# A fifth head-sum term moved from TensorE to GpSimd, and the value head sums in five batches

## The chip, the cores and the metric

The kernel runs on one core of a Trainium2 chip. The core has five engines with a queue of their own each: TensorE (PE in the profile, with its weight loads as PEld), VectorE (DVE), ScalarE (ACT), GpSimd (POOL) and SyncE (SP, which only issues transfers). The metric is the device time in microseconds of one execution of the whole program; lower is better. Three executions of the kernel before took 267.02, 267.12 and 267.43 us, median 267.12 us. On this kernel about 0.2% (0.53 us) is what a measurement can tell from no change.

## The reference

Two layers share one input of 2048 rows of 640 numbers, and their results are added to it:

```python
xn = _layernorm(x, axis=-1)
qkv = (xn @ wqkv)                      # 32 heads of 20, for q, k and v
# each position looks at 8 positions: itself and 2, 4, ... 14 rows back
logits = einsum("bhsd,bhswd->bhsw", q, kg) * 20 ** -0.5   # rows before 0 masked
o = einsum("bhsw,bhswd->bhsd", softmax(logits), vg)
h = (xn @ w_gate) * (xn @ w_up)        # 640 -> 1536
return x + o @ wo + h @ w_down
```

The dense products fill TensorE. The local attention is elementwise work: for each of the 8 offsets, q is multiplied by the shifted k, and the 20 products of a head are summed.

## The kernel before, in words

The 2048 rows are cut into four blocks of 512 (`NJ = 4`, `JB = 512`), and the 640 columns into five chunks of 128 partitions (`NCH = 5`). Columns are permuted so that in every chunk four neighbouring partitions belong to one head; a head's 20 numbers are four partitions in each of five chunks.

**Logits.** The 8 offsets are two groups of four, `r = 1` and `r = 0`. For one block, one group and one chunk, VectorE writes a tile of products (`PRD`, 128 x 4 x 512 in bf16, line 879, in `narrow`). TensorE then sums over partitions with the 128 x 32 matrix `G`: each product tile costs four matmuls, one for each stretch of 128 rows, into four column strips of one PSUM bank (line 994, in `logits`). For blocks 0 and 1 all ten tiles of a block (five chunks, two groups) go this way, 40 matmuls a block. Blocks 2 and 3 (`QUAD`) are different: only chunk 4 is made by `narrow`; the chunks 0 to 3 are multiplied straight out of PSUM by VectorE into FP32 half tiles (`PRF`, 128 x 2 x 512, line 926, in `wide`; `q0` = 0 or 2 names the half), and these are added up before TensorE sees them. `sum32` adds one half to another, by a GpSimd instruction (line 952) or, for the pairs in `BY_DMA`, by a transfer that accumulates (line 948), and `close` adds the last two and writes a bf16 half (line 970). So one group of a block gives two tiles to TensorE, the sum of four chunks and chunk 4 alone: four tiles a block. Blocks 2 and 3 are summed in one go (`JOIN`), 32 matmuls.

**Softmax** runs over pairs of blocks, on VectorE with the exponential on ScalarE (`softmax`, lines 1027 to 1054).

**Values.** For each unit `u` (block j, chunk c; 20 units), VectorE multiplies the shifted values by the weights (line 1173), GpSimd adds pairs of offsets (line 1178, two instructions a unit, tile `SV`), and TensorE sums the four groups of 32 partitions with `SEL` (line 1231, four matmuls a unit, in `sums`). The head sums are made in batches of five units, after unit 4, 9, 14 and 19 (`BATCH`). ScalarE copies the result to `OT`.

**Dense layers.** `gu` multiplies by the gate and up weights, for each block twelve pairs of five matmuls (line 1287); the two halves are multiplied by VectorE (lines 1296 and 1334). `dn` multiplies by the down weights and adds the attention's output product, 12 and 5 matmuls for each piece of 320 columns (line 1389). Units of block j must be summed before the pieces of block j can end.

**What sets the order.** Nothing runs dynamically. A planner (`Sched`) runs when the program is built: each step is a `Task` with an engine, a priority, the PSUM banks that it needs and the banks that must stay free beside them (`keep`). The planner has an assumed duration for each step and places the step that can start first on its engine, by priority. What comes out is one fixed order for each engine, with semaphore waits between them. So a change to a priority, a `keep` or an assumed duration changes the order of instructions on several engines. `GU_KEEP = 3` banks are held back from the gate and up products and `DN_KEEP = 5` from the down products, for the head sums. VectorE instructions whose operands all lie in SBUF and GpSimd's additions are kept apart in time (`lock=True`).

Of the kernel before, what the change touches and what calls it, by code (L numbers as in the profile page):

```python
# [11 lines left out]
NCH = 5  # L12
# [37 lines left out]
class Sched:  # L50
# [184 lines left out]
    def run(self):  # L235
        while self.threads:
            alive = []
            i = 0
            while i < len(self.threads):
                th = self.threads[i]  # L240
                if th[1] is not None or self._advance(th):
                    alive.append(th)
                i += 1
            self.threads = alive
            best = {}
            free = sorted((t, b) for b, t in self.banks.items() if t is not None)
            for th in self.threads:
                k = th[1]
                if k is None:
                    continue  # L250
                if k.banks and k.banks + k.keep > len(free):
                    continue
                got = self.choose(k, free)
                if k.banks and not got:
                    continue
                s = max([self.t[k.eng], k.ready] + [self.banks[b] for b in got])
                if k.lock:
                    s = max(s, self.t_lock)
                best.setdefault(k.eng, []).append((s, k, th))
            if not best:  # L260
                if self.threads:
                    raise RuntimeError(f"stuck: {len(self.threads)} threads at {self.t} banks {self.banks}")
                break
            pick = None
            for eng, c in best.items():
                lim = max(self.t[eng], min(x[0] for x in c)) + self.PATIENCE[eng]
                x = min((x for x in c if x[0] <= lim), key=lambda x: (x[1].prio, x[1].seq))
                if pick is None or x[0] < pick[0]:
                    pick = x
            _, k, th = pick  # L270
            th[1] = None
            if k.banks:
                got = self.choose(k, free)
                for b in got:
                    self.banks[b] = None
                k.emit(*got)
            else:
                k.emit()
# [77 lines left out]
def build_kernel(nc, A_x, A_wqkv, A_wo, B_x, B_w_gate, B_w_up, B_w_down, out):  # L356
# [65 lines left out]
    PRD += [sb("PRD12", [128, 4, JB], at=a_sc), sb("PRD13", [128, 4, JB], at=a_sc + 4096)]  # L422
    PRD32 = [K.sbuf(f"PRF{i}", [128, 2, JB], FP32, K.base[p.name]) for i, p in enumerate(PRD)]
    QUAD = {2: (1, 0), 3: (1, 0)}
    BY_DMA = (((0, 0), (0, 2)), ((1, 0), (1, 2)))
    a_xr = place[0]
    FB0 = sb("FB0", [128, 5, D])
# [32 lines left out]
    def mark(*k):  # L460
        done.add(k)
# [4 lines left out]
    def have(*k):  # L466
        return lambda: k in done
# [367 lines left out]
    def tokens():  # L835
        return []
# [7 lines left out]
    def products():  # L844
        rows = {j: [] for j in range(NJ)}
        joined = []
        holds = {}
        for at, (j, kind) in enumerate(ORDER):
            if kind == "w":
                if j not in holds:  # L850
                    yield from fetch(j, 0, holds.setdefault(j, {c: [] for c in range(4)}))
                yield from wide(j, rows[j], holds[j])
            else:
                if len(QUAD.get(j, ())) == 2 and j not in holds and (j, "w") == ORDER[at + 1]:
                    yield from fetch(j, 0, holds.setdefault(j, {c: [] for c in range(4)}))
                for r in (1, 0):
                    for c in range(NCH - 1 if r in QUAD.get(j, ()) else 0, NCH):
                        yield from narrow(j, r, c, rows[j])
            if len(rows[j]) == 10 - 3 * len(QUAD.get(j, ())):
                if j in JOIN:  # L860
                    joined.append((j, rows[j]))
                    if len(joined) == len(JOIN):
                        K.spawn(logits(*joined))
                else:
                    K.spawn(logits((j, rows[j])))
        mark("products")
# [42 lines left out]
    def wide(j, slots, hold):  # L909
        halves = [(r, q0) for r in QUAD[j] for q0 in (0, 2)]  # L910
        acc, parts = {}, {1: [], 0: []}
        for c0 in (0, 2):
            for i, (r, q0) in enumerate(halves):
                f = []
                for c in (c0, c0 + 1):
                    yield lambda: len(hold[c]) > 0 and len(usable(j)) > 0
                    yield num(4, "qk", 0, j, c)
                    k = slot(j)
                    f.append(k)
                    o = PRD32[k]  # L920
                    kv, rk = k_view(j, r, c, q0, 2)
                    q = PS[:, hold[c][0], :]
                    qb = q.unsqueeze(1).to_broadcast([128, 2, JB])

                    def go(o=o, qb=qb, kv=kv, q=q, rk=rk):
                        X = op("dve", lambda e: e.tensor_tensor(o[:], qb, kv, ALU.mult), r=[q, rk, ("qev", j, c)], w=[o[:]],  # L926
                               name=f"prow{j}_{r}_{c}_{q0}", occ=1.17)
                        if c == 3:
                            mark("prow", j, r, q0)
                        if (r, q0) == halves[-1]:  # L930
                            K.free_bank(hold[c][0], X)

                    yield Task("dve", go, r=[q, rk], w=[o[:]], prio=20 + j)
                    if c == 2:
                        K.spawn(close(j, r, q0, acc, f, parts[r]))
                if c0 == 0:
                    acc[r, q0] = f[0]
                    K.spawn(sum32(j, r, q0, 0, *f))
                if i == len(halves) - 2 and c0 == 0:
                    yield from fetch(j, 2, hold)  # L940
        for r in QUAD[j]:
            slots.append((acc[r, 0], PRD[acc[r, 0]], r, parts[r]))

    def sum32(j, r, q0, p, a, b):
        x, y = PRD32[a][:], PRD32[b][:]
        name = f"qsum{j}_{r}_{q0}_{p}"
        if (r, q0) in BY_DMA[p]:
            yield Task("pool", lambda: op("pool", lambda e: e.dma_start(x, y, accum_op=ALU.add), r=[x, y], w=[x], dma=True,
                                          name=name, occ=0.88, acc=3.4), r=[x, y], w=[x], prio=4)
        else:  # L950
            yield calm
            yield Task("pool", lambda: op("pool", lambda e: e.tensor_tensor(x, x, y, ALU.add), r=[x, y] + tokens(), w=[x],  # L952
                                          name=name, occ=2.36, lock=True), r=[x, y], w=[x], prio=5, lock=True)
        free.append(b)

    def close(j, r, q0, acc, f, parts):
        A = acc[r, q0]
        a, x, o = PRD32[A][:], PRD32[f[0]][:], PRD[acc[r, 0]][:, q0:q0 + 2, :]
        if (r, q0) in BY_DMA[1]:
            yield have("prow", j, r, q0)  # L960
            yield from sum32(j, r, q0, 1, *f)
            y = x
        else:
            yield from sum32(j, r, q0, 1, A, f[0])
            yield have("prow", j, r, q0)
            y = PRD32[f[1]][:]
        if q0:
            yield lambda: len(parts) == 1
        yield calm
        yield Task("pool", lambda: op("pool", lambda e: e.tensor_tensor(o, a, y, ALU.add), r=[a, y] + tokens(), w=[o],  # L970
                                      name=f"qend{j}_{r}_{q0}", occ=2.36, lock=True), r=[a, y], w=[o], prio=5, lock=True)
        free.append(f[0] if (r, q0) in BY_DMA[1] else f[1])
        if q0:
            free.append(A)
        parts.append(q0)
# [108 lines left out]
        yield Task("sp", move, r=[L[:]], prio=4)  # L1084

    NU = NJ * NCH
    BATCH = (4, 9, 14, 19)

    def vx_loads():
        yield have("products")  # L1090
# [128 lines left out]
    def sums(us):  # L1219
# [5 lines left out]

        def go(*bs):
            hold.extend(bs)
            for u, b in zip(us, bs):
                for dq in range(4):
                    o, p = PS[32 * dq:32 * dq + 32, b, :], SV[sv_of[u]][:, dq, :]  # L1230
# [25 lines left out]
        return count.get(("lg",), 0) >= NJ and m < 11 and ucount[0] - count.get(("hp",), 0) < HP_MAX  # L1256

    SEQ = [(0, range(NF)), (1, range(6)), (2, (0, 1, 2, 3, 8, 9, 10, 11)), (1, range(6, NF)), (2, range(4, 8)), (3, range(NF))]

    def gu():  # L1260
        for m in range(NCH):
# [4 lines left out]
        for j, m in [(j, m) for j, ms in SEQ for m in ms]:  # L1266
# [73 lines left out]
                yield num(k0, "hf")  # L1340
                yield Task("dve", fmul, r=[h, us], prio=H_PRIO, lock=True)

            yield Task("pe", lambda b: go(0, b), prio=50, banks=1, keep=GU_KEEP, r=[WG[:]])
            K.spawn(after())
            yield Task("pe", lambda b: go(1, b), prio=49, banks=1, keep=GU_KEEP - 1, r=[WU[:]])
            bump("gus", j)
            if count["gus", j] == NF:
                mark("gu", j)
# [24 lines left out]
    def dn_piece(j, t, nb, rows, c0, c1):  # L1373
# [60 lines left out]
            if nb == 1:  # L1434
                mark("out", t)

        yield Task("pe", down, prio=41, banks=1, keep=0 if count.get(("ot", j), 0) >= NCH else DN_KEEP, r=[WD[:], WO[:]])
        K.spawn(tail())

    FAST = [(1, m) for m in range(6, NF)] + [(2, m) for m in range(4, 8)]  # L1440
# [11 lines left out]
    ORDER = ((0, "n"), (1, "n"), (2, "n"), (3, "n"), (2, "w"), (3, "w"))  # L1452
    LAST = ORDER[-1][0]
    HP_PRIO = 30
    DN_KEEP = 5
    H_PRIO = 9
    FIN_PRIO = 8

# [75 lines left out]
```

## Time and profile before

| | |
|---|---|
| median of three executions | 267.12 us (267.02 to 267.43) |
| profiled execution, first to last instruction (span) | 265.2 us, granted clock 1.000 |
| median less that span (start and end around it) | 1.9 us |
| VectorE busy | 220.0 us (83%) |
| GpSimd busy | 143.8 us (54%) |
| ScalarE busy | 111.8 us (42%) |

The profiled execution is an execution of its own; it is known by its span of 265.2 us, and its time is taken as that span and the 1.9 us around it. In the profile's timeline a row is a run of neighbouring instructions on one engine: the start, the length, the engine, the line, what is written and read, how many, and in brackets how long the engine had been idle and who ended that. In the table of groups, the columns behind the count are busy time, mean nanoseconds of one instruction, and idle time just before them. TensorE's matmuls overlap, so the length of a row is somewhat more than the distance to the next row's start; distances between starts are used below for what a row costs.

### The profile page before, as it was taken

The numbers are of one execution on the slowest core, as the hardware profiler recorded it, in microseconds if no ns is written. First come the engines' busy times: TensorE is split into PE (matmuls) and PEld (weight loads), VectorE is DVE, ScalarE is ACT, GpSimd is POOL, SyncE is SP. The second block draws the span as 40 slices with busy tenths as digits, with TensorE's granted clock in tenths as the row PEclk, the third lists the DMA queues.
The fourth block names the chain that finished last, engine by engine and source line by source line (L and its number), as shares of the span: only waits on it lengthen the run. The fifth ranks groups of instructions, "written<-read, shape, count | busy, mean of one in ns | idle before, by whom it ended". The sixth has DMA issues, their size and how long they took to land.

```text
span 265.2 us, 4403 instructions
## 1 busy us (share of the span) xinstructions
PE 259.5 (98%) x1748; PEld 152.5 (58%) x1764; DVE 220.0 (83%) x259; ACT 111.8 (42%) x203; POOL 143.8 (54%) x89
## 2 busy tenths in 40 slices
PE   7999999999999999999999999999999999999996
PEld 5996965444444444444444444477557755775675
DVE  4687899999998699667999999999999989992212
ACT  3559987556612211224267653511442144211300
POOL 3000000000644996169973476799999989997000
DMA  7974679960479994840069734453893657004211
GB/s 206 371 220 82 123 126 394 394 247 2 126 148 188 236 215 82 162 79 1 4 167 317 151 77 114 95 149 98 223 198 84 155 109 159 2 0 61 41 49 52
DMA packets 39685, 37.84 MB, mean 143 GB/s; under 512 B 15696, under 2 KB 37328, under 8 KB 39632
## 3 DMA queue, kind: packets, MB, share of 16 engines
q1 hardware_dynamic: 36688, 31.32, 44.0%
q0 software_dynamic: 2736, 6.16, 13.6%
q8 instruction: 14, 0.23, 0.4%
q10 hardware_dynamic: 240, 0.07, 0.1%
q14 instruction: 7, 0.06, 0.1%
HBM read 25.07 MB, written 7.23 MB: 122 GB/s over the span
## 4 chain that ended last, share of the span: by engine, by line
PE 89%; ACT 5%; DVE 3%; issue 2%; DMA 1%; DVEq 0%
PE PS L1287 37%; PE PS L1389 28%; PE PS L697 17%; ACT XNS L608 3%; PE PS L994 2%; PE PS L729 2%; PE PS L1231 1%; DVE PV L1173 1%; DMA XST<-in_A_x_dram 1%; DVE XNT L1296 1%; ACT QT L702 1%; ACT VST L702 1%; ACT KT L702 1%; PE PS L641 1%; ACT SD L583 0%
## 5 line engine op out<-in xcount | busy, mean ns | idle before, releaser
L1178 POOL TENSOR_TENSOR SV<-PV 128x1024 bf16<-128x1024 f32 x40 | 94.7, 2463 | 16.0 <-DVE HT L1334 7.8
L1173 DVE TENSOR_TENSOR PV<-VX,PS 128x1024 f32<-128x1024 bf16 (+1 forms) x54 | 90.6, 1725 | 0.6 <-POOL SV L1178 0.5
L697 PE MATMUL PS<-XNT,WQKV 128*128 128x512 bf16 (+2 forms) x384 | 60.0, 315 | 0.5 <-issue 0.3
L1287 PE MATMUL PS<-XNT,WU 128*128 128x512 bf16 x239 | 59.4, 379 | 0.1
L1287 PE MATMUL PS<-XNT,WG 128*128 128x512 bf16 x231 | 57.7, 379 | 0.6 <-issue 0.2
L697 PEld LDWEIGHTS PS<-XNT,WQKV 128*128 128x128 bf16 x390 | 37.8, 112 | 21.9 <-ACT LOG L1005 0.8
L1287 PEld LDWEIGHTS PS<-XNT,WU 128*128 128x128 bf16 x240 | 23.5, 98 | 28.1
L1287 PEld LDWEIGHTS PS<-XNT,WG 128*128 128x128 bf16 x240 | 23.4, 98 | 28.1 <-ACT LOG L1005 0.4
L926 DVE TENSOR_TENSOR PRF<-PS,KT 128x1024 f32<-128x1024 f32 x32 | 37.9, 1216 | 0.3 <-PE PS L697 0.3
L952 POOL TENSOR_TENSOR PRF<-PRF,PRF 128x1024 f32<-128x1024 f32 x8 | 18.8, 2358 | 21.6 <-DVE LOG L1054 20.6
L702 ACT ACTIVATE HT<-PS 128x512 bf16<-128x512 f32 x24 | 14.3, 596 | 35.3 <-PE PS L1287 35.3
L1389 PE MATMUL PS<-WD,HT 128*128 128x320 bf16 x192 | 28.4, 299 | 0.5 <-DVE XNT L1296 0.5
L702 ACT ACTIVATE FB<-PS 128x320 bf16<-128x320 f32 x24 | 10.5, 438 | 40.5 <-PE PS L1389 40.5
L879 DVE TENSOR_TENSOR PRD<-QT,KT 128x2048 bf16<-128x2048 bf16 x24 | 27.3, 1218 | 0.0
L1389 PE MATMUL PS<-WO,OT 128*128 128x320 bf16 (+2 forms) x165 | 26.3, 295 | 0.0
L1013 POOL MEMSET LOG<- 32x6 bf16 (+6 forms) x7 | 0.4, 95 | 43.8 <-ACT LOG L1005 43.8
L1389 PEld LDWEIGHTS PS<-WD,HT 128*128 128x128 bf16 x192 | 18.6, 98 | 8.5 <-DVE XNT L1296 1.0
L970 POOL TENSOR_TENSOR PRD<-PRF,PRF 128x1024 bf16<-128x1024 f32 x8 | 19.0, 2396 | 0.9 <-DVE PRF L926 0.8
L1389 PEld LDWEIGHTS PS<-WO,OT 128*128 128x128 bf16 x165 | 16.0, 98 | 5.8
L1296 DVE TENSOR_TENSOR HT<-HT,PS 128x512 bf16<-128x512 bf16 x18 | 12.3, 685 | 8.1 <-PE PS L1287 8.1
L1402 DVE TENSOR_TENSOR FB<-PS,XR 128x320 bf16<-128x320 f32 (+2 forms) x9 | 4.1, 455 | 14.9 <-PE PS L1389 14.9
L573 DVE BATCH_NORM_STATS2 STATS<-XST 128x6 f32<-128x320 bf16 x32 | 14.1, 470 | 2.2 <-DMA XST<-in_A_x_dram 2.2
(71 smaller groups left out, 233.4 us busy)
## 6 DMA issues: line engine op xcount, KB each, us to landing
VX<-v_scratch SPq DMA_DIRECT2D x80, 130.0 KB, 2.9
PRF<-PRF POOLq DMA_DIRECT2D x8, 512.0 KB, 4.9
XST<-in_A_x_dram SPq DMA_DIRECT2D x16, 160.0 KB, 5.6
v_scratch<-VST SPq DMA_DIRECT2D x4, 640.0 KB, 5.6
WG<-in_B_w_gate_dram SPq DMA_DIRECT2D x1, 1920.0 KB, 8.4
WU<-in_B_w_up_dram SPq DMA_DIRECT2D x1, 1920.0 KB, 12.0
out_dram<-in_A_x_dram SPq DMA_DIRECT2D x1, 1920.0 KB, 19.4
WD<-in_B_w_down_dram SPq DMA_DIRECT2D x1, 1920.0 KB, 8.7
```

The costliest lines, as they stand in the source:

```text
L573: op("dve", lambda e: e.bn_stats(o, a), r=[a], w=[("st", t, i)], name=f"bn{t}_{i}", occ=0.49)
L697: op("pe", (lambda o, l, x, c, first: lambda e: e.matmul(o, l, x, start=first, stop=(c == NCH - 1)))(o, l, x, c, first), r=[l, x], w=[o], ...
L702: X = op("act", (lambda o, i: lambda e: e.activation(o, i, ACT.Copy))(o, i), r=[i], w=[o], name=name, occ=0.12 + n * 0.9e-3)
L879: op("dve", lambda e: e.tensor_tensor(s[:], qb, kv, ALU.mult), r=[q, rk], w=[s[:]], name=f"prod{j}_{r}_{c}", occ=1.15, lock=True)
L926: X = op("dve", lambda e: e.tensor_tensor(o[:], qb, kv, ALU.mult), r=[q, rk, ("qev", j, c)], w=[o[:]], name=f"prow{j}_{r}_{c}_{q0}", occ=1.17)
L952: yield Task("pool", lambda: op("pool", lambda e: e.tensor_tensor(x, x, y, ALU.add), r=[x, y] + tokens(), w=[x], name=name, occ=2.36, lock ...
L970: yield Task("pool", lambda: op("pool", lambda e: e.tensor_tensor(o, a, y, ALU.add), r=[a, y] + tokens(), w=[o], name=f"qend{j}_{r}_{q0}", ...
L1173: last[0] = op("dve", lambda e: e.tensor_tensor(p, vw, a, ALU.mult), r=[vv] + rk, w=[p], name=f"pv{u}_{x}_{r0}", occ=0.09 + 1.1 * nr)
L1178: X = op("pool", lambda e: e.tensor_tensor(o, p[:, :, 0, :], p[:, :, 1, :], ALU.add), r=[p[:]] + tokens(), w=[o], name=f"pva{u}_{x}", occ= ...
L1287: op("pe", (lambda l, x, c: lambda e: e.matmul(PS[:, b, :], l, x, start=(c == 0), stop=(c == NCH - 1)))(l, x, c), r=[l, x], w=[PS[:, b, :] ...
L1296: X = op("dve", lambda e: e.tensor_tensor(h, h, PS[:, hold[1], :], ALU.mult), r=[h, PS[:, hold[1], :]], w=[h], name=f"h{m}_{j}", occ=0.65)
L1389: op("pe", (lambda l, x, i: lambda e: e.matmul(dst, l, x, start=(i == 0), stop=(i == n - 1)))(l, x, i), r=[l, x], w=[PS[:, b, :]], name=f" ...
```

## The change

Three things are changed.

1. In blocks 2 and 3 the product of chunk 4 no longer goes to TensorE as a tile of its own. `sum32` adds it, half by half, into the FP32 sum of chunks 0 and 1, by one more GpSimd addition (FP32 and bf16 in, FP32 out; `LAST_DMA` is empty, so none goes by transfer). `close` waits for it in the planner. There are eight such additions: two blocks, two groups, two halves. The head sums of blocks 2 and 3 then have one tile a group, 16 matmuls where there were 32.
2. `BATCH` has five entries: the last five units are summed as three (15, 16, 17) and two (18, 19).
3. The banks held back follow the head sums: `reserve` holds none back in some phases, and the down products keep as many banks free as the next batch has units (`next_sums`) in place of five.

In the built program GpSimd has eight instructions more, TensorE 16 matmuls fewer; VectorE, ScalarE and SyncE have the same instructions in another order. TensorE's order differs in four places: the order of one gate/up pair beside a group of line 697; the place of the 16 matmuls among the gate/up pairs of the second block, with as many pairs ahead of them as before; one gate group in the first two batches' wake ahead of the down products and its up group behind them; and at the end, where the three remaining gate/up groups come earlier, the batch of three stands before the down products of the last block, and the batch of two stands behind 36 of their matmuls (before: one batch of five behind 12).

```diff
@@ Sched.run
-                if k.banks and k.banks + k.keep > len(free):
+                if k.banks and k.banks + (k.keep() if callable(k.keep) else k.keep) > len(free):
@@ build_kernel
     QUAD = {2: (1, 0), 3: (1, 0)}
+    LAST_DMA = ()
     BY_DMA = (((0, 0), (0, 2)), ((1, 0), (1, 2)))
@@ products
-            if len(rows[j]) == 10 - 3 * len(QUAD.get(j, ())):
+            if len(rows[j]) == 10 - 4 * len(QUAD.get(j, ())) and kind == ("w" if j in QUAD else "n"):
@@ wide
         acc, parts = {}, {1: [], 0: []}
+        lastc = {r: [n, 0] for n, _, r in slots}
+        slots.clear()
...
-                    K.spawn(sum32(j, r, q0, 0, *f))
+                    K.spawn(sum32(j, r, q0, 0, *f, last=lastc[r]))
...
-    def sum32(j, r, q0, p, a, b):
+    def sum32(j, r, q0, p, a, b, last=None):
...
         free.append(b)
+        if last is None:
+            return
+        z = PRD[last[0]][:, q0:q0 + 2, :]
+        if (r, q0) in LAST_DMA:
+            yield Task("pool", lambda: op("pool", lambda e: e.dma_start(x, z, accum_op=ALU.add), r=[x, z], w=[x], dma=True,
+                                          name=name + "c", occ=0.88, acc=3.4), r=[x, z], w=[x], prio=4)
+        else:
+            yield calm
+            yield Task("pool", lambda: op("pool", lambda e: e.tensor_tensor(x, x, z, ALU.add), r=[x, z] + tokens(), w=[x],
+                                          name=name + "c", occ=2.36, lock=True), r=[x, z], w=[x], prio=5, lock=True)
+        last[1] += 1
+        mark("sum", j, r, q0)
+        if last[1] == 2:
+            free.append(last[0])
@@ close
         if q0:
             yield lambda: len(parts) == 1
+        yield have("sum", j, r, q0)
         yield calm
@@ build_kernel
-    BATCH = (4, 9, 14, 19)
+    BATCH = (4, 9, 14, 17, 19)
@@ sums, go
             hold.extend(bs)
+            bump("sums")
@@ build_kernel
+    def next_sums():
+        n = count.get(("sums",), 0)
+        return BATCH[n] - (BATCH[n - 1] if n else -1) if n < len(BATCH) else 0
+
+    def reserve(n):
+        k = sum(("add", u) in done for u in range(NU))
+        return 0 if k % 5 < 2 and k else n
@@ gu
-            yield Task("pe", lambda b: go(0, b), prio=50, banks=1, keep=GU_KEEP, r=[WG[:]])
+            yield Task("pe", lambda b: go(0, b), prio=50, banks=1, keep=lambda: reserve(GU_KEEP), r=[WG[:]])
             K.spawn(after())
-            yield Task("pe", lambda b: go(1, b), prio=49, banks=1, keep=GU_KEEP - 1, r=[WU[:]])
+            yield Task("pe", lambda b: go(1, b), prio=49, banks=1, keep=lambda: reserve(GU_KEEP) - 1 if reserve(GU_KEEP) else 0, r=[WU[:]])
@@ dn_piece
-        yield Task("pe", down, prio=41, banks=1, keep=0 if count.get(("ot", j), 0) >= NCH else DN_KEEP, r=[WD[:], WO[:]])
+        yield Task("pe", down, prio=41, banks=1, keep=0 if count.get(("ot", j), 0) >= NCH else next_sums, r=[WD[:], WO[:]])
@@ build_kernel
-    DN_KEEP = 5
```

## The prediction

> **What bounds the kernel now.** I read the page's busy shares first, then the chain that ended last, then the timelines of TensorE and GpSimd where the change lies. The busy shares and the clock:
>
> ```profile
> PE 259.5 (98%) x1748; PEld 152.5 (58%) x1764; DVE 220.0 (83%) x259; ACT 111.8 (42%) x203; POOL 143.8 (54%) x89
> core 0: 265.2 us, clock 1.000
> ```
>
> TensorE is the bound, at full clock: what is taken from its queue is gained, as long as nothing it waits for comes late. The chain, in order of time, shows the head sums of blocks 2 and 3 on it, and the one place behind them where TensorE isn't what ends last:
>
> ```profile
> 133.81 1.84 PE PS L994 x32
> ...
> 157.39 5.36 PE PS L1287 x24
> 162.75 0.66 DVE XNT L1296
> ...
> 169.05 0.69 DVE XNT L1296
> 169.74 0.05 issue
> 169.78 18.65 PE PS L1389 x136
> ```
>
> The reader is to see 32 matmuls in 1.84 us (0.0575 us each), and that from 162.75 to 169.74 VectorE sets the pace. TensorE's timeline shows what that is worth, and what a batch of value head sums costs:
>
> ```profile
> 168.06 1.26 PE L1231 MATMUL PS<-SV,SEL 128*32 128x512 bf16 x20
> 169.78 3.43 PE L1389 MATMUL PS<-WD,HT 128*128 128x320 bf16 x24 [0.46 <-DVE XNT L1296]
> ...
> 194.84 1.26 PE L1231 MATMUL PS<-SV,SEL 128*32 128x512 bf16 x20
> 196.03 3.43 PE L1389 MATMUL PS<-WD,HT 128*128 128x320 bf16 x24
> ...
> 244.65 1.26 PE L1231 MATMUL PS<-SV,SEL 128*32 128x512 bf16 x20
> 245.84 3.43 PE L1389 MATMUL PS<-WD,XNT 128*128 128x320 bf16 x24
> ```
>
> From start to start the batches at 194.84 and 244.65 take 1.19 us, that at 168.06 takes 1.72: 0.53 us is a wait. GpSimd's timeline shows what room the eight new additions find:
>
> ```profile
> 82.07 0.86 POOL L948 DMA_DIRECT2D PRF<-PRF  x1 [3.53 <-DVE PRF L926]
> ...
> 97.72 4.68 POOL L952 TENSOR_TENSOR PRF<-PRF,PRF 128x1024 f32<-128x1024 f32 x2
> 102.34 0.82 POOL L948 DMA_DIRECT2D PRF<-PRF  x1
> ...
> 114.45 0.86 POOL L948 DMA_DIRECT2D PRF<-PRF  x1 [5.62 <-DVE PRF L926]
> ...
> 127.92 2.35 POOL L970 TENSOR_TENSOR PRD<-PRF,PRF 128x1024 bf16<-128x1024 f32 x1
> 130.22 4.71 POOL L1178 TENSOR_TENSOR SV<-PV 128x1024 bf16<-128x1024 f32 x2
> ...
> 241.44 2.86 POOL L1178 TENSOR_TENSOR SV<-PV 128x1024 bf16<-128x1024 f32 x1
> ```
>
> **The change part by part.**
>
> *Matmuls removed.* 16 of line 994 at 0.0575 us, on TensorE, on the path: −0.92 us. Bounds: 0 if TensorE then waits for GpSimd there, 16 x 0.0575 otherwise. The stop and start around the group (0.09 us ahead of 133.74) stay.
>
> *Eight additions on GpSimd.* One distance is 2.31 us (97.72 to 102.34 is two): 18.5 us more work between 68.70 and 130.22. GpSimd's idle times in that stretch, all waits for VectorE's products, are 0.25, 2.25, 3.53, 0.83, 1.91, 2.05, 5.62 and 0.87: 17.3 us. If all of it is filled, GpSimd comes to the value additions 1.2 us later; if none, 18.5. The new additions stand in the order between the transfers and additions that did the waiting, so I am near the first: 1 us of waits stays for the first half tiles of block 3, which VectorE still makes when it did, and the shift is 2.2 us. Its cover, place by place:
> - The logits. The last `close` ended at 130.27 and ends at 132.5; TensorE reaches line 994 after as many matmuls as before, at 133.74. 1.2 us are left. If that cover goes, TensorE waits with all gate and up pairs queued behind it.
> - The softmax of the second pair follows the same evacuation on ScalarE, which doesn't move. VectorE's value products wait for `PV` buffers that GpSimd frees, 2.2 us later at first. From 130.22 to 169.21 GpSimd is idle 15.5 us (0.42, 4.35, 3.47, 1.74, 0.87, 0.61, 2.34, 1.65), mostly for VectorE multiplications kept apart from it, so the shift can be caught up there. TensorE reaches the first batch of value sums later itself: one more gate/up pair ahead of it, twice the 1.08 us from the group at 165.81 to that at 166.89, less 0.92: 169.3 instead of 168.06. GpSimd's additions for that batch ended at 167.56. If the shift is caught up, 1.7 us are left; if all of it were carried, TensorE would wait 0.5.
> - The last batch. From 169.21 on GpSimd has little idle time, so the shift may carry to its last addition, 244.30 + 2.2 = 246.5. TensorE came to that batch at 244.65, 18.3 us before its last matmuls began (262.9). Now 24 matmuls that stood behind it stand ahead (245.84 to 249.11, 3.27 us), and 12 value sums with them (0.69): 14.3 us before an end at 261.8, so 247.5. 1.0 us is left, against 0.35 before.
>
> So the additions cost nothing by this sum. Their duration is the unknown: an addition of FP32 and bf16 into FP32 is not in the trace. The rows around it:
>
> ```profile
> L970 POOL TENSOR_TENSOR PRD<-PRF,PRF 128x1024 bf16<-128x1024 f32 x8 | 19.0, 2396 | 0.9 <-DVE PRF L926 0.8
> L952 POOL TENSOR_TENSOR PRF<-PRF,PRF 128x1024 f32<-128x1024 f32 x8 | 18.8, 2358 | 21.6 <-DVE LOG L1054 20.6
> L926 DVE TENSOR_TENSOR PRF<-PS,KT 128x1024 f32<-128x1024 f32 x32 | 37.9, 1216 | 0.3 <-PE PS L697 0.3
> ```
>
> Between 2.35 (the shortest two-operand addition of the trace on GpSimd) and 2.87 (the longest, one with a transfer's issue beside it). I take 2358 ns, the row with the same output and first operand; the type of the output moves it by 38 ns. The lower end gains nothing, since GpSimd isn't the bound; the upper end is the rival that ends slower.
>
> The Trainium skill speaks against this part: GPSIMD Engine Reference, section "Engine selection", says to keep elementwise work on a tile off GpSimd, which is about twice as slow with two inputs. The rows agree on the ratio (2358 against 1216 ns for as many numbers on VectorE). By the page's 4497 ns for 2048 numbers, the eight would be an estimated 18.0 us and not 18.5, and the sum the same. The rule would make of the change a loss only where GpSimd's time is the path's; the 17.3 us idle say it isn't.
>
> *The wait at 169.78.* VectorE's last gate multiplication freed a bank 0.53 us late. Now a gate group stands ahead of the down products there, and TensorE arrives 1.24 us later, while VectorE has one more multiplication to do by then (0.6 us): 0.64 us of lateness taken off. That would clear all of 0.53, but VectorE's value products are themselves held by the later GpSimd. Ends: 0 and −0.53; I take −0.35.
>
> *The fifth batch.* A batch of 20 takes 1.19 us and its matmuls 1.15; with the 0.10 ahead of it (the up group at 193.66 would end its 1.08 at 194.74) a batch more costs 0.15 us. Ends: 0.05 and 0.25.
>
> *Banks held back and order.* The gate and up groups moved are the same matmuls, and a bank held longer by a lone gate group is one of eight. SyncE's order differs only in four value loads, of unit 6, that now stand behind the sixteen transfers of the second pair's attention weights and not ahead; VectorE needs unit 6 at 170.78, and those transfers were issued from 151.95 to 162.2; four loads and 2.9 us to landing end by 167, 3.8 us ahead of need. I cost this at nothing; its ends are the 0.53 that one late bank cost in this trace, either way.
>
> **Sum**: −0.92 − 0.35 + 0.15 = −1.12 us. The profiled execution's span goes from 265.2 to 264.1; with the same 1.9 us around it, the median from 267.12 to 266.0.
>
> **The rivals.**
> 1. *The new additions are longer than the FP32 ones and the logits wait (slower).* Cover at line 994 is 1.2 us, 0.15 for each of eight. From 2.51 us each TensorE waits; each further 0.1 costs 0.8 us; the 1.12 is gone at 2.65, and from 2.72 on the kernel is measurably slower. At 2.87 each: 8 x 0.51 − 1.2 = 2.9, so 268.9 us. For it: the form isn't in the trace. Against it: all three forms that are lie within 2.36 to 2.46 in the mean.
> 2. *GpSimd's shift is larger than 2.2 and shows at the first or last batch.* At 3.2 to 3.7 us of shift it costs 0.5 to 1 us: 266.5 to 267.0. For it: from 169 us on nothing is idle on GpSimd. Against it: 15.5 us idle ahead of that.
> 3. *New waits for banks or for VectorE.* Another order, with fewer banks held back, gives one or two waits of 0.53, and the old one stays: 267.0 to 267.8. For it: VectorE is busy 33.78 of the 36 us from 134 to 170. Against it: the batches at 194.84 and 244.65 show no wait now.
>
> **How the numbers follow.** Forecast 0.64 (its own range 265.7 to 266.4: the wait from 0 to −0.53, the batch from 0.05 to 0.25); rival 1 0.10; rival 2 0.18; rival 3 0.08. 0.2% is 0.53 us, what a measurement of this kernel can tell from no change. Faster: the forecast and 0.08 of rival 2, 0.72. Same: the rest of rival 2 and half of rival 3, 0.14. Slower: rival 1 and half of rival 3, 0.14. The range is 265.4 to 267.6: below, both order terms at their good ends (−0.92 − 0.53 + 0.05 − 0.3); above, rivals 2 and 3, with rival 1 left out.
>
> **What would show it.** Right: 16 matmuls in some 0.92 us at line 994 at the same start, without idle time before it that GpSimd ended; the new additions at 2.36 us; the first value addition at 132.4; no wait, or under 0.2, behind the first batch; the last value addition done before TensorE's batch at 247.5. Wrong: additions over 2.5 us, idle time before line 994 or 1231 put down to GpSimd, or a row of line 1389 or 1287 waiting for VectorE by more than 0.5 us.

## The result and the profile after

The changed kernel takes 266.25 us (median of 22 runs, 265.75 to 267.75) where the kernel before takes 267.21 us beside it (22 runs, 266.9 to 267.5). The ratio is 0.9972, with a 95% interval of 0.9964 to 0.998: faster by about 1.0 us. The prediction was 266.0 us.

A run's time has two parts, the span from first to last instruction and a rest around it. Before, the span is 265.5 us in the median of the 59 runs beside the experiments below, with a rest of 1.67 to 1.89. The changed kernel's 22 runs have a median span of 264.35, 21 of them from 264.0 to 264.6 and one 266.0, with a rest of 1.70 to 2.93. So most of the spread of its times lies outside the span. In spans it is 1.15 us faster.

The busy shares of the changed kernel:

```profile
PE 259.8 (98%) x1748; PEld 151.8 (57%) x1748; DVE 220.1 (83%) x259; ACT 111.9 (42%) x203; POOL 160.8 (61%) x97
core 0: 264.4 us, clock 1.000
```

GpSimd has 17.0 us more, VectorE and ScalarE are as they were, and the span is 0.8 us shorter. TensorE's count of matmuls reads 1748 in both profiles although 16 were taken out, so matmul records are missing from the trace of before (its weight loads read 1764, now 1748), and the sums below go by starts, not by busy time. The chain that ended last, in order of time, at the places that the prediction spoke of:

```profile
8.74 2.99 PE PS L730 x50
...
134.22 0.98 PE PS L1012 x16
...
169.83 1.19 PE PS L1250 x20
171.03 1.19 PE PS L1314 x5
172.21 18.47 PE PS L1416 x136
...
242.10 0.76 PE PS L1250 x12
242.86 5.00 PE PS L1416 x36
247.86 0.55 PE PS L1250 x8
248.40 13.75 PE PS L1416 x117
...
262.17 0.29 DVE FB L1429
```

Line 994 is now 1012: 16 matmuls in 0.98 us where there were 32 in 1.84. From 162.75 to 169.74, where VectorE set the pace before, there is now TensorE alone, and its first batch of value sums (line 1231, now 1250) is followed by the next matmul without a gap.

The first row shows what the span hides. TensorE's 50 matmuls of line 730 (729 before) began at 8.74, against 8.33 in the profile of before, because the second load of `x` landed late; that 0.41 us has nothing to do with the change. I therefore compare a stretch that leaves the start out, from the start of these 50 matmuls to the start of the last result on VectorE: 262.94 − 8.33 = 254.61 us before, 262.17 − 8.74 = 253.43 after, **1.18 us less**. "The stretch" below is this measure.

GpSimd's timeline around the new additions (line 966), the value additions (line 1196) and the end:

```profile
78.10 0.86 POOL L951 DMA_DIRECT2D PRF<-PRF  x1 [0.34 <-DVE PRF L929]
78.66 4.54 POOL L966 TENSOR_TENSOR PRF<-PRF,PRD 128x1024 f32<-128x1024 f32 x2
82.83 1.20 POOL L951 DMA_DIRECT2D PRF<-PRF  x1
83.44 2.75 POOL L966 TENSOR_TENSOR PRF<-PRF,PRD 128x1024 f32<-128x1024 f32 x1
85.53 2.96 POOL L955 TENSOR_TENSOR PRF<-PRF,PRF 128x1024 f32<-128x1024 f32 x1
87.84 2.95 POOL L988 TENSOR_TENSOR PRD<-PRF,PRF 128x1024 bf16<-128x1024 f32 x1
...
100.89 0.87 POOL L951 DMA_DIRECT2D PRF<-PRF  x1 [0.86 <-DVE PRF L929]
...
110.55 0.87 POOL L951 DMA_DIRECT2D PRF<-PRF  x1 [1.12 <-DVE PRF L929]
...
132.57 4.68 POOL L1196 TENSOR_TENSOR SV<-PV 128x1024 bf16<-128x1024 f32 x2
...
243.96 2.86 POOL L1196 TENSOR_TENSOR SV<-PV 128x1024 bf16<-128x1024 f32 x1
```

Of the 17.3 us that GpSimd waited for VectorE's products, 0.34 + 0.86 + 1.12 = 2.3 us are left; the additions lie in the rest. Its first value addition comes at 132.57 (130.22 before), and its last ends at 246.82, just before TensorE's last batch:

```profile
242.03 0.83 PE L1250 MATMUL PS<-SV,SEL 128*32 128x512 bf16 x12
242.80 5.06 PE L1416 MATMUL PS<-WD,XNT 128*128 128x320 bf16 x36
247.79 0.61 PE L1250 MATMUL PS<-SV,SEL 128*32 128x512 bf16 x8
```

### The profile page after: what moved, and what is told of

Same layout as the page of the kernel before. It is cut to its first block, busy times and chain, and to the rows that moved or that the text cites. A ratio compares the mean times of both kernels' runs of the same rounds, so it can differ in the third digit from the quotient of the medians.

```text
span 264.4 us, 4405 instructions
## 1 busy us (share of the span) xinstructions
PE 259.8 (98%) x1748; PEld 151.8 (57%) x1748; DVE 220.1 (83%) x259; ACT 111.9 (42%) x203; POOL 160.8 (61%) x97
## 4 chain that ended last, share of the span: by engine, by line
PE 96%; DMA 2%; DVE 1%; SPq 0%; ACT 0%; issue 0%
PE PS L1314 39%; PE PS L1416 28%; PE PS L698 23%; PE PS L1012 2%; PE PS L1250 2%; PE PS L730 2%; DMA XST<-in_A_x_dram 2%; DVE STATS L574 0%; PE PS L642 0%; SPq L480 0%; ACT XNT L655 0%; DVE XNS L603 0%; ACT SD L584 0%; DVE FB L1429 0%; DVE MV L577 0%
## 5 line engine op out<-in xcount | busy, mean ns | idle before, releaser
L698 PE MATMUL PS<-XNT,WQKV 128*128 128x512 bf16 (+2 forms) x390 | 60.8, 316 | 0.0
L1314 PE MATMUL PS<-XNT,WG 128*128 128x512 bf16 x240 | 59.7, 379 | 0.0
L955 POOL TENSOR_TENSOR PRF<-PRF,PRF 128x1024 f32<-128x1024 f32 x8 | 22.0, 2755 | 20.6 <-DVE LOG L1072 20.6
L988 POOL TENSOR_TENSOR PRD<-PRF,PRF 128x1024 bf16<-128x1024 f32 x8 | 21.5, 2768 | 0.1
L966 POOL TENSOR_TENSOR PRF<-PRF,PRD 128x1024 f32<-128x1024 f32 x8 | 19.5, 2543 | 0.0
```

The source lines that it names most:

```text
L698: op("pe", (lambda o, l, x, c, first: lambda e: e.matmul(o, l, x, start=first, stop=(c == NCH - 1)))(o, l, x, c, first), r=[l, x], w=[o], ...
L1314: op("pe", (lambda l, x, c: lambda e: e.matmul(PS[:, b, :], l, x, start=(c == 0), stop=(c == NCH - 1)))(l, x, c), r=[l, x], w=[PS[:, b, :] ...
```

## The experiments

My theory: the 16 matmuls and the wait behind the first batch are the gain, the fifth batch is a small loss, GpSimd's work is free, and the order and the banks count for nothing. Against it: that the order or the banks carry the gain, or that the time depends on GpSimd.

In what follows "the stretch" is compared with the 254.61 us of before. The kernel before was run again beside each group of experiments, with medians of 267.27, 267.3 and 267.28 us.

### The additions alone, with the old banks and four batches

```diff
-    BATCH = (4, 9, 14, 17, 19)
+    BATCH = (4, 9, 14, 19)
@@ gu
-            yield Task("pe", lambda b: go(0, b), prio=50, banks=1, keep=lambda: reserve(GU_KEEP), r=[WG[:]])
+            yield Task("pe", lambda b: go(0, b), prio=50, banks=1, keep=GU_KEEP, r=[WG[:]])
-            yield Task("pe", lambda b: go(1, b), prio=49, banks=1, keep=lambda: reserve(GU_KEEP) - 1 if reserve(GU_KEEP) else 0, r=[WU[:]])
+            yield Task("pe", lambda b: go(1, b), prio=49, banks=1, keep=GU_KEEP - 1, r=[WU[:]])
@@ dn_piece
-        yield Task("pe", down, prio=41, banks=1, keep=0 if count.get(("ot", j), 0) >= NCH else next_sums, r=[WD[:], WO[:]])
+        yield Task("pe", down, prio=41, banks=1, keep=0 if count.get(("ot", j), 0) >= NCH else 5, r=[WD[:], WO[:]])
```

> The eight additions alone: four batches, three and five banks held back as before. Theory A (the prediction's sum; banks and order cost nothing): -0.92 for the 16 matmuls and -0.35 to -0.53 for the wait behind the first batch, no fifth batch: 265.8 us, ratio to the kernel before 0.9946 to 0.9953. Theory B (the change of the held banks is what lets TensorE use the removed work): the built order puts the third batch of value sums right ahead of the five output products that need its copies, and the gate/up pairs that stood there are used up; TensorE then waits for ScalarE's copies five times by 0.2 to 0.35 us, and the gain is gone: 267.2 to 267.5, ratio 1.000 to 1.001, with idle time of line 1416 put down to line 1258's copies on ScalarE near 224 us.

Measured: 267.53 us (266.86 to 268.39, 12 runs), ratio 1.0014 (1.0002 to 1.0026). The stretch is 254.54 us, 0.07 shorter than before. The additions by themselves gain nothing. Yet the first batch runs without its wait here too, so 0.92 + 0.53 were gained and some 1.4 lost elsewhere. TensorE's timeline shows where, at the third batch:

```profile
223.68 1.26 PE L1250 MATMUL PS<-SV,SEL 128*32 128x512 bf16 x20
224.88 0.70 PE L1416 MATMUL PS<-WO,OT 128*128 128x320 bf16 x2
225.76 0.31 PE L1416 MATMUL PS<-WO,OT 128*128 128x320 bf16 x1 [0.18 <-ACT OT L1259]
226.25 0.31 PE L1416 MATMUL PS<-WO,OT 128*128 128x320 bf16 x1 [0.18 <-ACT OT L1259]
226.74 0.31 PE L1416 MATMUL PS<-WO,OT 128*128 128x320 bf16 x1 [0.18 <-ACT OT L1259]
226.89 1.25 PE L1416 MATMUL PS<-WD,HX 128*128 128x320 bf16 x8
```

and the chain at the same place names the engine that it waits for:

```profile
223.75 0.36 PE PS L1250 x4
...
224.13 1.44 ACT OT L1259 x3
...
225.58 1.12 ACT OT L1259 x2
...
226.74 19.73 PE PS L1416 x144
```

The output products (`WO`) stand right behind the batch whose results they read, and each has to wait for ScalarE's copy into `OT`. Unhindered, the fifth would have started four distances of 0.136 us (the eight matmuls from 226.89 to 227.98 take 1.09) after 224.88, at 225.42; it started at 226.74: **1.3 us** lost, of the 1.4. In the kernel before and in the changed one, 24 matmuls of the down weights stand between the batch and the first output product, 3.27 us in the changed kernel:

```profile
223.45 1.26 PE L1416 MATMUL PS<-WD,HX 128*128 128x320 bf16 x8
...
226.72 1.52 PE L1416 MATMUL PS<-WO,OT 128*128 128x320 bf16 x10
```

### The order without the additions

```diff
-            if len(rows[j]) == 10 - 4 * len(QUAD.get(j, ())) and kind == ("w" if j in QUAD else "n"):
+            if len(rows[j]) == 10 - 3 * len(QUAD.get(j, ())):
@@ wide
-        slots.clear()
...
-                    K.spawn(sum32(j, r, q0, 0, *f, last=lastc[r]))
+                    K.spawn(sum32(j, r, q0, 0, *f))
@@ close
-        yield have("sum", j, r, q0)
```

> The five batches and the banks held back as in the change, without the eight additions. Theory A (part by part): +0.15 for the fifth batch, the wait behind the first batch kept, since GpSimd and VectorE come when they did: 267.3, ratio 1.0003 to 1.001. Rival (the change gains by its order, not by the matmuls): -0.5 us or more, ratio under 0.998. The wait of 0.5 us is still there near 169.6 us, now before a gate group instead of a down product.

Measured: 267.47 us (267.26 to 267.88, 11 runs), ratio 1.0006 (0.9997 to 1.0015); the stretch is 0.21 longer than before. The wait behind the first batch is still there, now ahead of the gate group:

```profile
168.28 1.26 PE L1248 MATMUL PS<-SV,SEL 128*32 128x512 bf16 x20
170.00 1.25 PE L1312 MATMUL PS<-XNT,WG 128*128 128x512 bf16 x5 [0.46 <-DVE XNT L1321]
```

So a gate group behind the batch doesn't remove that wait by itself. In the kernel with the additions alone it is gone with the down products standing straight behind the batch, as before. What the two kernels without the wait have in common is one more gate/up pair ahead of the batch (16 and not 15 since the head sums), so that TensorE gets there 1.3 us later (169.76 − 0.41 against 168.06 in the changed kernel). Without the additions the planner doesn't place that pair there, so this kernel has only a part of the changed kernel's order; the runs with short additions and with the matmuls put back, below, have all of it.

### The change with four batches

```diff
-    BATCH = (4, 9, 14, 17, 19)
+    BATCH = (4, 9, 14, 19)
```

> The whole change, but the last five units summed in one batch. Theory A: without the fifth batch's 0.15 us, 266.1, ratio 0.9964 or a little under the changed kernel's 0.9972. Rival (the fifth batch is needed since GpSimd's last addition comes late): GpSimd's last addition ended at 246.8 in the changed kernel's trace and the one batch would stand at about 246.7 to 247: a wait of 0 to 0.5 us, 266.3 to 266.7, ratio 0.997 to 0.9985.

Measured: 265.88 us (265.63 to 267.35, 6 runs), ratio 0.9955 (0.9937 to 0.9973); the stretch is 1.40 shorter than before, 0.22 shorter than with five batches. Here GpSimd's last addition ends only just in time for TensorE's batch:

```profile
243.79 2.85 POOL L1196 TENSOR_TENSOR SV<-PV 128x1024 bf16<-128x1024 f32 x1
...
246.74 1.26 PE L1250 MATMUL PS<-SV,SEL 128*32 128x512 bf16 x20
```

That is 246.64, 0.10 us ahead of the batch that needs it. The fifth batch widens that margin to 0.97 us, at the price of 0.2, and the margin isn't needed.

### The additions and five batches, with the old banks

The edit is that of the first experiment without its line on `BATCH`.

> The additions and the five batches, with the banks held back as before. Theory A (held banks cost nothing): as the changed kernel, 266.2, ratio 0.997. Theory B (the held banks decide): the waits for ScalarE's copies behind the third batch as with the additions alone, and one batch more: 267.4 to 267.7, ratio 1.0005 to 1.002.

Measured: 267.92 us (267.13 to 270.53, 12 runs), ratio 1.0037 (1.0016 to 1.0058); the stretch is 0.14 longer than before. It shows the same stop at the third batch as the first experiment, in the chain:

```profile
224.51 1.27 ACT OT L1259 x3
...
227.12 16.48 PE PS L1416 x120
```

Between this kernel and the changed one lies nothing but the rule for the banks, and it is worth 0.14 + 1.18 = 1.3 us of the stretch. This execution's granted clock reads 0.998; that its stretch is 0.21 longer than that of the first experiment, as one batch more would make it (0.22), speaks against a part of the clock in the 1.3. The span of 267.6 us has a further 1.7 us in it behind the last result, where the last 32 KB store took 3.2 us to land and the changed kernel's took 1.4; that is not TensorE's, and no part of the comparison above.

### The new additions made short

```diff
-            yield Task("pool", lambda: op("pool", lambda e: e.tensor_tensor(x, x, z, ALU.add), r=[x, z] + tokens(), w=[x],
+            yield Task("pool", lambda: op("pool", lambda e: e.tensor_tensor(x[:, :, 0:8], x[:, :, 0:8], z[:, :, 0:8], ALU.add), r=[x, z] + tokens(), w=[x],
                                           name=name + "c", occ=2.36, lock=True), r=[x, z], w=[x], prio=5, lock=True)
```

> The changed kernel with the same order on every engine, but each of the eight new additions covers 16 of 1024 columns (so most of chunk 4's product is left out of the sums): GpSimd gets back some 17 us. Theory A (GpSimd's additions lie wholly beside TensorE's work): as the changed kernel, 266.2, ratio 0.996 to 0.998. Rival (they cost something on the path, and their late ends are what spreads the changed kernel's times over 265.75 to 267.75): 265.8 or less, ratio 0.995, and a spread under 0.6 us.

Measured: 266.02 us (265.88 to 266.37, 5 runs), ratio 0.9959 (0.9945 to 0.9972); the stretch is 1.17 shorter than before, as in the changed kernel. With nearly all of the added work gone from GpSimd the time is the same, so that work costs nothing. It doesn't even move GpSimd much:

```profile
74.18 0.52 POOL L966 TENSOR_TENSOR PRF<-PRF,PRD 128x16 f32<-128x16 f32 x1
...
77.81 0.86 POOL L951 DMA_DIRECT2D PRF<-PRF  x1 [2.24 <-DVE PRF L929]
...
128.85 4.67 POOL L1196 TENSOR_TENSOR SV<-PV 128x1024 bf16<-128x1024 f32 x2
```

The waits for VectorE's products come back, and the first value addition is at 128.85 instead of 132.57, 3.7 us earlier (3.4 by the start of the stretch, at 8.44 here).

### The 16 matmuls put back

```diff
+                        if j in QUAD:
+                            op("pe", (lambda o, x, a: lambda e: e.matmul(o, G[:], x, start=True, stop=True, tile_position=(0, 32 * a)))(o, x, a),
+                               r=[G[:], x], w=[o], name=f"lx{j}_{r}_{i}_{a}", occ=0.0, lat=0.4, mode=1)
                         op("pe", (lambda o, x, i, a, nt: lambda e: e.matmul(o, G[:], x, start=(i == 0), stop=(i == nt - 1),
```

> The changed kernel with the same order, but each of the 16 head-sum matmuls of blocks 2 and 3 is issued twice (the first result is overwritten), so TensorE has the 32 of before. Theory A: +0.92 us, 267.2, ratio 0.9995 to 1.001. Rival (the gain is the order's and the cleared wait's, not the matmuls'): under +0.3, ratio 0.997 to 0.998.

Measured: 267.22 us (266.69 to 267.34, 11 runs), ratio 0.9993 (0.9984 to 1.0002). That is 0.97 us over the changed kernel's 266.25 and 1.13 over its 266.09 of the repeat below, and in the stretch 0.88 (254.31 against 253.43); the prediction's term is 0.92. The matmuls are on the path and cost what they take. The chain at the first batch shows what is left of the gain with all 32 matmuls:

```profile
170.99 1.19 PE PS L1253 x20
172.18 1.19 PE PS L1317 x5
```

The wait behind the batch is gone here too, and so it is in the kernel with short additions (1.20 us from the batch at 169.46 to the gate group at 170.66). Neither the matmuls taken out nor GpSimd's work is what clears it, then, but the order that the two share with the changed kernel. That order is worth 0.30 us of the stretch: the 0.53 of the wait, less the 0.22 of the fifth batch.

### More GpSimd work: one addition, and three

One more addition of 128 x 1024 numbers, into a tile that nothing reads, ahead of the first new one; then three, ahead of three of the four new ones of block 2 (the condition is then `j == 2 and (r, q0) != (0, 2)`). The planner's clock is set back behind each, so that no engine's order moves.

```diff
+            def cadd():
+                if (j, r, q0) == (2, 1, 0):
+                    t0, tl = K.t["pool"], K.t_lock
+                    op("pool", lambda e: e.tensor_tensor(UX[:, 0:2, :], x, x, ALU.add), r=[x] + tokens(), w=[UX[:, 0:2, :]], name=name + "d", occ=0.0, lock=True)
+                    K.t["pool"], K.t_lock = t0, tl
+                op("pool", lambda e: e.tensor_tensor(x, x, z, ALU.add), r=[x, z] + tokens(), w=[x],
+                   name=name + "c", occ=2.36, lock=True)
```

> The changed kernel with the same order, but one more GpSimd addition of 128 x 1024 (2.31 us, into a tile nobody reads) ahead of the first of the eight. By the prediction's cover of 1.2 us at the head sums: +1.1 us, 267.3, ratio 1.000. By the changed kernel's own trace (GpSimd's last close ends 1.5 us ahead of TensorE's head sums, and 2.3 us of idle time on GpSimd lie between): 0 to +0.2, 266.2 to 266.4, ratio 0.997 to 0.998.

> The same with three more additions of 2.31 us (6.9 us), all in block 2. By the prediction's cover of 1.2 us: +5.7, 272, ratio 1.018. By the trace's 1.5 and 2.3: +3.1, 269.3, ratio 1.008, with TensorE idle ahead of the 16 head-sum matmuls. If TensorE doesn't depend on GpSimd there: 266.3.

Measured with one: 266.04 us (265.82 to 266.13, 5 runs), ratio 0.9954 (0.9941 to 0.9966), no slower than the change. GpSimd has caught up by its first value addition, at 132.22; this execution's stretch starts at 8.36, so that is 132.60 by the start of the changed kernel's, against 132.57. Measured with three: 268.42 us (268.27 to 268.58, 5 runs), ratio 1.0044 (1.0031 to 1.0056), 2.4 us slower than with one. Three distances of 2.31 are 6.9 us, so 4.5 of them were covered: both expectations, 5.7 and 3.1 us slower, were too high. TensorE's timeline with three shows two of the places that pay:

```profile
134.64 0.83 PE L1020 MATMUL PS<-PRD,G 128*32 128x512 bf16 x12
136.08 0.40 PE L1020 MATMUL PS<-PRD,G 128*32 128x512 bf16 x4 [0.61 <-POOL PRD L996]
...
171.05 1.65 PE L1258 MATMUL PS<-SV,SEL 128*32 128x512 bf16 x20
173.35 1.25 PE L1322 MATMUL PS<-XNT,WG 128*128 128x512 bf16 x5 [0.64 <-DVE XNT L1331]
```

The first is the prediction's cover at line 994 gone: `close` is late for the last four matmuls. The second is the first batch, which then waits again, for VectorE. The stretch of this execution is 2.6 us longer than the changed kernel's. Between starts the first place costs 0.8 us more (136.64 − 134.64 = 2.0 against 135.13 − 134.15 = 1.0, less 0.2 for the record of one matmul of five that is missing), the second 1.1 (173.35 − 171.05 = 2.3 against 170.96 − 169.76 = 1.2). The other 0.7 are in small stops before 107 us, whose cause I didn't follow.

### The change and the four batches once more, and half of the rule for the banks

The changed kernel and the kernel with four batches were run again on one chip, beside a kernel with five batches in which only the down products follow the new rule:

```diff
@@ gu
-            yield Task("pe", lambda b: go(0, b), prio=50, banks=1, keep=lambda: reserve(GU_KEEP), r=[WG[:]])
+            yield Task("pe", lambda b: go(0, b), prio=50, banks=1, keep=GU_KEEP, r=[WG[:]])
-            yield Task("pe", lambda b: go(1, b), prio=49, banks=1, keep=lambda: reserve(GU_KEEP) - 1 if reserve(GU_KEEP) else 0, r=[WU[:]])
+            yield Task("pe", lambda b: go(1, b), prio=49, banks=1, keep=GU_KEEP - 1, r=[WU[:]])
```

> The changed kernel itself, beside the next three on one chip, since its 22 runs spread over 265.75 to 267.75 while the kernels with the same additions and one more or 16 more matmuls spread over 0.3 to 0.7 us. If the spread is the kernel's own, it shows again, median 266.2; if it was that of the chips it ran on, under 0.7 us, median 266.1.

> The change with the last five units in one batch, again, on the same chip as the changed kernel. Theory A: one batch less is 0.15 us less, 265.9 to 266.0, ratio 0.995 to 0.996.

> The change with the gate and up products' three and two banks held back as before (without reserve), the down products keeping as many banks as the next batch has units. Theory B1 (five banks held back from the down products are what kept the gate and up pairs running ahead and used them up, and the units of the next batch suffice): 266.2 to 266.3, ratio 0.996 to 0.997. Theory B2 (reserve is what decides): as with the additions and five batches and the old banks, 267.5 to 267.9, ratio 1.001 to 1.004.

Measured: the change 266.09 us (265.94 to 266.9, 5 runs), ratio 0.9963 (0.9951 to 0.9976); four batches 265.87 us (265.61 to 266.18, 5 runs), ratio 0.9946 (0.9934 to 0.9959); the half rule 266.08 us (266.0 to 266.19, 5 runs), ratio 0.9956 (0.9944 to 0.9968).

Four batches are ahead of five by 0.22 us in the medians, with intervals that overlap. In the stretch it is again 0.22 against the changed kernel's first profile, and 0.38 against the one of this repeat, which lost 0.16 before 15 us. The half rule is as fast as the change: with five batches `next_sums` alone does it. TensorE's timeline of that kernel at the third batch:

```profile
223.83 1.26 PE L1250 MATMUL PS<-SV,SEL 128*32 128x512 bf16 x20
225.03 1.26 PE L1416 MATMUL PS<-WD,HX 128*128 128x320 bf16 x8
```

Down products follow, and ScalarE's copies have time. With four batches `next_sums` gives five until the last batch is placed, the same as the old constant; by the code it must there be `reserve` that keeps the third batch in good order. So `next_sums` is enough with five batches and `reserve` with four (`reserve` alone with five wasn't run), and with neither the stop of 1.3 us is there.

### A further step: two more pairs of tiles added before TensorE

On the kernel with four batches, the tiles of chunks 0 and 1 (group `r = 1`) in blocks 0 and 1 are added to each other by an accumulating transfer, so that TensorE has eight head-sum matmuls less.

```diff
+    PAIRS = ((0, 1, 1), (1, 1, 1))
...
+    def pair(j, r, c, a, b, p):
+        x, y = a[1][:], b[1][:]
+        yield Task("pool", lambda: op("pool", lambda e: e.dma_start(x, y, accum_op=ALU.add), r=[x, y], w=[x], dma=True,
+                                      name=f"pair{j}_{r}_{c}", occ=0.88, acc=3.4), r=[x, y], w=[x], prio=4)
+        free.append(b[0])
+        p.extend((0, 1))
```

> A further step along the same way: four batches, and in blocks 0 and 1 the products of chunks 0 and 1 of group r = 1 are added by an accumulating transfer each (GpSimd's queue is idle there), so eight matmuls of the head sums less. If matmuls taken off TensorE are gained as before: 8 x 0.0575 = 0.46 us under the kernel with four batches, 265.5, ratio 0.9935 to 0.9945. If the transfers land late (up to 7.5 us in the changed kernel's trace), TensorE waits ahead of the head sums of block 0 or 1: 266 to 268.

Measured: 266.19 us (265.37 to 267.14, 10 runs), ratio 0.996 (0.9947 to 0.9974). The chain of its profile:

```profile
3.24 6.32 DMA XST<-in_A_x_dram
...
15.03 30.47 PE PS L699 x240
```

From the start of these 240 matmuls to the last result it is 0.43 us faster than the kernel with four batches (246.72 against 247.15), about 8 matmuls of 0.0575. TensorE reaches the head sums of blocks 0 and 1 without idle time, so the late transfers of the second expectation cost nothing in this execution. But it began late: a load of `x` ended at 9.56 us. The gain isn't seen in the median, which missed the first expectation by 0.7 us. The times of this kernel spread over 1.8 us, and here, unlike with the change, the spans do (263.6 to 265.4); the cause wasn't settled.

## Why the prediction was right, point by point

**Matmuls removed (−0.92): right.** The group starts at 134.15, which is 133.74 and the late start of 0.41, and is 0.86 us shorter in the chain; doubling the matmuls again costs 0.97 (0.88 in the stretch).

**Eight additions at no cost: right, with the size of the term wrong in both directions.** Their distance is 2.09 us (83.44 to 85.53; two in 4.17 from 78.66 to 82.83), below the lower end of 2.35 that I gave, and below the FP32 pairs' 2.31 (85.53 to 87.84). Their recorded durations have a mean of 2543 ns, over the 2.5 us that I had set as a sign of being wrong; but these records overlap (last section), and the distance is what GpSimd's queue paid. So 16.7 us were added and not 18.5. With 15.0 of idle time used up, 1.7 are left of a forecast shift of 2.2; measured is 132.57 − 0.41 − 130.22 = 1.9. The place with least cover was the first batch: its additions end at 169.11 (164.44 and 4.67 in GpSimd's timeline), 0.65 us ahead of TensorE, where I had named 1.7 for a shift that is caught up and a wait of 0.5 for one that isn't. The last value addition ends 0.97 us before its batch starts, forecast 1.0 (the 262.9 in that sum is where the last matmuls end, not where they begin; the sum itself holds). **Rival 1** (additions over 2.5 us) fell by that distance; its price was also too high. I let each microsecond beyond 1.2 cost one, but one more addition of 2.3 us costs nothing and three of 6.9 cost 2.4: the idle time that is left between the added work and TensorE's head sums (2.3 us here) absorbs as well. **Rival 2** fell with the same runs.

The rule that the Trainium skill gives (GPSIMD Engine Reference, section "Engine selection": keep elementwise work on a tile off GpSimd) didn't decide here. The run with short additions is the test: 266.02 us without nearly all of that work, 266.09 with it.

**The wait behind the first batch (−0.35): right in direction, mis-sized.** All of 0.53 is gone. I had computed 0.64 us of lateness removed, and took off a part for VectorE being held by GpSimd; no run shows that, short of three additions too many. The reason is the one given, that TensorE arrives later: the wait stays in the order-only run, which has the gate group behind the batch but not the pair ahead of it, and is gone with short additions and with the matmuls put back.

**The fifth batch (+0.15): right.** 0.2 measured, inside its ends.

**"Banks held back and order ... I cost this at nothing": right as a term of the sum, wrong in its reason**, which the total hides. From before to after, nothing appears at these places, so zero fits the account as a whole. But I had taken the order of before as the one that the additions would have without the rest, and that isn't so: with the additions and the old banks, the planner puts output products right behind the third batch, and TensorE stands for 1.3 us. The new rule is worth that, 2.5 times the ±0.53 that I gave as its ends, and more than the 0.92 of the matmuls. Rival 3 named this kind of wait, but in the changed kernel and for VectorE; it came in a kernel that has only half of the change, and for ScalarE.

Put together, in the stretch: −0.92 (matmuls) − 0.53 (wait) + 0.15 (batch) = −1.30, measured −1.18; with the measured 0.86 and 0.22 for the first and the last it is −1.17. By experiment: additions alone −0.07, with the new rule for the banks and four batches −1.40, with the fifth batch −1.18.

**The total.** The sum of −1.12 from 267.12 gave 266.0; measured are −0.96 in one group of runs and −1.19 in the repeat, and −1.15 in spans. That the sum comes so near is in part luck: the wait was 0.18 short one way, and the matmuls (0.06) and the batch (0.07) were off the other way. The 1.9 us around the span, taken over unchanged, was right in the median of the changed kernel's runs, but they reach 2.93. The loads of `x` and the last store lie inside the span, so they aren't the cause; the kernel with the additions alone has a rest of up to 2.94, and the kernels with short additions, one more or three more of at most 1.98. Where it comes from stays open.

## What to carry to other kernels

When a bounding engine gives work away, its arrival everywhere behind moves, and a planner may put the next consumer straight behind its producer: look at each place where the bounding engine reads what another engine has just copied, and compare the order with each half of the change, since one half may only pay for the other. An idle engine's cover is not the margin at the nearest consumer alone, but that margin together with the idle time left between the added work and that consumer; add dummy work in steps to measure it. Compare the spans of the runs before their times, since the rest around the span can spread more than the change is worth. Split the spans of two profiles at the first row that doesn't depend on how the first loads landed, or a difference of 0.4 us in the start reads like a part of the change.

## What the runs showed that I had not expected

- On GpSimd an addition with one bf16 operand (FP32 and bf16 in, FP32 out, 128 x 1024) takes 2.09 us from start to start, the same with two FP32 operands 2.31.
- Durations of GpSimd instructions that follow each other without a gap overlap in the records, so they don't add up. The two groups of the changed kernel read 2755 and 2768 ns at a distance of 2.31 us, where those of before read 2358 and 2396 at the same distance; what makes the records of the changed kernel longer isn't shown. The new additions read 2543 ns at 2.09 us:

```profile
L955 POOL TENSOR_TENSOR PRF<-PRF,PRF 128x1024 f32<-128x1024 f32 x8 | 22.0, 2755 | 20.6 <-DVE LOG L1072 20.6
L988 POOL TENSOR_TENSOR PRD<-PRF,PRF 128x1024 bf16<-128x1024 f32 x8 | 21.5, 2768 | 0.1
L966 POOL TENSOR_TENSOR PRF<-PRF,PRD 128x1024 f32<-128x1024 f32 x8 | 19.5, 2543 | 0.0
```
